# A weight's sign by ScalarE's parametric ReLU, and the norm's factor by one product

## The chip, the cores and the metric

The kernel runs on one core of a Trainium2 chip. The metric is device time in microseconds (us), the median of the runs shown. TensorE multiplies matrices, VectorE and ScalarE work elementwise, GpSimd (POOL in the profile) sets constants and helps with sums, and SyncE (SP) issues the DMAs.

## The reference, cut to what matters

Three stages follow one another, all in float32 at the interface:

```python
# 1. linear attention: batch 8, heads 8, sequence 576, head width 64
kv  = einsum('bhsd,bhse->bhde', k, v)
out = einsum('bhsd,bhde->bhse', q, kv)
rms = sqrt(mean(out * out, axis=-1, keepdims=True) + 1e-06)
x   = (out / rms * g_norm)               # -> 4608 tokens x 512
# 2. gated product
h   = ((x @ w1) * (x @ w2)) @ w3         # 512 -> 1024 -> 1024
x   = h @ w_out                          # 1024 -> 512
# 3. SiLU block
h   = x @ w_in                           # 512 -> 2048
out = (h / (1 + exp(-h))) @ w_out2       # 2048 -> 512
```

Two facts of it touch the change. Every weight matrix reaches the kernel as float64 (pairs of 32-bit words), so the kernel converts each weight to float32 itself. And the root mean square is one number per token and head, which has to be spread over the 64 features of its head before it multiplies `out`.

## The kernel before, in words

**Precision.** A large product runs in three passes on rounded operands: each operand is split into a high part (a ScalarE copy to a rounded type) and a low part (VectorE: operand minus high part), and TensorE adds high*high, high*low and low*high (`passes`, L111). Every pass is 128x128 weights against 128x512 columns.

**Conversion of weights.** The weights come in pieces of 128x512 values, 512 KB each, 72 in all. `advance` (L293) moves a pipeline of pieces by one step and writes the instructions of several pieces in this order: the DMA of piece n+3 (`cv_load`, L154), the high part of piece n-1 on ScalarE (`cv_high`, L207), two scaling operations of piece n+1 on ScalarE (`cv_scale`, L161), the joining of bits of piece n on VectorE (`cv_bits`, L194), and the low part of piece n-1 on VectorE (`cv_low`, L222). In `cv_scale` L169 makes `t` from the high words (scaled by 2^-112) and L170 makes `z` from the low words. In `cv_bits` L201 takes the sign bit of the high word from the raw tile and puts it into `z`, and L203 shifts `t` left by three bits and joins `z`. So VectorE does three operations a piece (L201, L203, the low part) and ScalarE three (L169, L170, the high part). The raw tile has three buffers, and a fourth for every fourth piece of the opening; it is free once its last reader is done, which is L201.

**Opening.** Up to about 88 us the kernel folds w3 and w_out into one matrix (`w_mm`, L476: 16 groups of 12 products, each group waiting for one or two fresh pieces), and fits in the first batches of `kv`, the first 512 tokens of the attention, and the first pieces of w1 and w2. `SLOTS` (L55) writes the order out by hand: it names after which piece each step of the attention stands.

**Middle.** From about 88 to 613 us the gated product runs over seven chunks of 512 tokens (products `pa`, `pb`, `x2ps`), and `event` and `att_step` (L585, L613) place the attention of the other chunks and the rest of the conversion between its products, again in an order written out by hand.

**End.** From there to the end the SiLU block and the remaining gated chunks run as seven-product block schemes (L796), whose weights are reloaded from memory.

**The norm.** For each of nine chunks: `att_c` sums squares with the constant matrix `ones`, so that rows 32p and 32p+1 of one bank hold the two heads of pair p; `att_d` and `att_e` make the factor `u` (ScalarE: Ln, Exp, Square; VectorE: two operations) and split it into `rh` (ScalarE) and `rl` (VectorE). `att_r` (L412), called twice a chunk, spreads it: for two pairs p, one product of 32 rows of `spread` with `rh` and one with `rl`, both into the same bank. `att_x` (VectorE) multiplies by it. `spread` holds -0.5 where a row belongs to a half, set by GpSimd before anything else runs (L128 to L136).

**Order.** Each engine works through its own instructions in the order in which they are written; an instruction that waits holds up all behind it on its engine. SP issues DMAs in the same way.

Of the kernel before, what the change touches and what calls it, by code (L numbers as in the profile page):

```python
# [7 lines left out]
F32 = mybir.dt.float32  # L8
F32R = mybir.dt.float32r
U32 = mybir.dt.uint32  # L10
AF = mybir.ActivationFunctionType
ALU = mybir.AluOpType
# [3 lines left out]
P = 128  # L16
B, H, S, D = 8, 8, 576, 64
# [5 lines left out]
N = 512  # L23
# [50 lines left out]
def fused(ctx, tc, q, k, v, g, w1, w2, w3t, wo1, wb, out):  # L74
# [3 lines left out]
    nc = tc.nc  # L78
    opened = {}

    def pool(name, **how):
        opened[name] = tc.tile_pool(name=name, **how)
        return opened[name].__enter__()
# [9 lines left out]
    const = pool(name="const", bufs=1, side="right")  # L93
# [10 lines left out]
    def bank(tag, bufs, name):  # L104
        return ps.tile([P, N], F32, tag=tag, bufs=bufs, name=name)

    def split(h, l, x):
        nc.scalar.copy(out=h, in_=x)  # L108
        nc.vector.tensor_sub(out=l, in0=x, in1=h.bitcast(F32))
# [11 lines left out]
    eps = const.tile([P, 1], F32)  # L121
    nc.gpsimd.memset(eps, EPS)
    ones = const.tile([P, 32], F32)
    const.tile([P, 80], F32, name="pad_left")
    spread = const.tile([P, P], F32R)
    kv32 = [const.tile([P, KD, D], F32, name=f"kv32_{i}") for i in range(2)]
    const.tile([P, 120], F32, name="pad_right")
# [1 line left out]
    nc.gpsimd.memset(spread.bitcast(F32), 0.0)  # L129
    for i in range(2):  # L130
        nc.gpsimd.memset(ones[i * D:(i + 1) * D, i:i + 1], 1.0)
    for p in range(KD):
        r = 32 * p
        nc.gpsimd.memset(spread[r:r + 2, D:].bitcast(F32), -0.5)
        nc.gpsimd.memset(spread[r:r + 1, D:].bitcast(F32), 0.0)
        nc.gpsimd.memset(spread[r:r + 1, :D].bitcast(F32), -0.5)  # L136

    wch = [wc.tile([P, N], F32R, name=f"wch{m}") for m in range(K1)]
    wcl = [wc.tile([P, N], F32R, name=f"wcl{m}") for m in range(K1)]
# [11 lines left out]
    stage = {}  # L151
# [9 lines left out]
    def cv_scale(n):  # L161

        if n < len(pieces) and pieces[n][0] is not None and pieces[n][1] != "sum":
            t = cv.tile([P, N], F32, tag="t", name=f"t{n}")
            z = cv.tile([P, N], U32, tag="z", bufs=2, name=f"z{n}")
            w = stage[n].rearrange("p (n two) -> p n two", two=2)
            nc.scalar.activation(out=t, in_=w[:, :, 1].bitcast(F32), func=AF.Copy, scale=2.0 ** -112)  # L169
            nc.scalar.activation(out=z, in_=w[:, :, 0], func=AF.Copy, scale=0.93 * 2.0 ** -29)  # L170
            stage[n] = stage[n], t, z

    def cv_sum(n):


        src, _, role, dst = pieces[n]
        t = cv.tile([P, N], F32, tag="t", name=f"t{n}")
        w = N // len(src)
        for x, halves in enumerate(src):
            h, l = (y.bitcast(F32) for y in halves)  # L180
            nc.vector.tensor_add(out=t[:, x * w:(x + 1) * w], in0=h, in1=l)
            for i, y in ((0, h), (1, l)):

                y0, at0 = (0, x * w) if role else (max(0, 2 * P - x * w), max(0, x * w - 2 * P))
                if y0 < w:
                    if w > 2 * P:
                        ops_ = dst[:, 1:3, i, :] if role else dst[:, 0:1, i, :]
                        nc.sync.dma_start(out=ops_, in_=y[:, y0:].rearrange("p (o c) -> p o c", c=2 * P))
                    else:
                        op = 1 + at0 // (2 * P) if role else 0  # L190
                        nc.sync.dma_start(out=dst[:, op, i, at0 % (2 * P):at0 % (2 * P) + w], in_=y)
        stage[n] = t

    def cv_bits(n):  # L194
        if n < len(pieces) and pieces[n][0] is not None and pieces[n][1] == "sum":
            cv_sum(n)
        elif n < len(pieces) and pieces[n][0] is not None:
            raw, t, z = stage[n]
            hi = raw.rearrange("p (n two) -> p n two", two=2)[:, :, 1]
            tu = t.bitcast(U32)  # L200
            nc.vector.scalar_tensor_tensor(out=z, in0=hi, scalar=0x80000000, in1=z,  # L201
                                           op0=ALU.bitwise_and, op1=ALU.bitwise_or)
            nc.vector.scalar_tensor_tensor(out=tu, in0=tu, scalar=3, in1=z,  # L203
                                           op0=ALU.logical_shift_left, op1=ALU.bitwise_or)
            stage[n] = t
# [87 lines left out]
    def advance():  # L293
        nonlocal done
        n = done
        flush()
        cv_load(n + 3)
        cv_high(n - 1)
        cv_scale(n + 1)
        cv_bits(n)  # L300
        block_sums(n)
        cv_low(n - 1)
        done += 1
# [8 lines left out]
    at = pool(name="at", bufs=1)  # L312
# [46 lines left out]
    r_t = {}  # L359
# [42 lines left out]
    def att_e(c):  # L402

        s, r, u = r_t[c]
        nc.vector.scalar_tensor_tensor(out=u, in0=s, scalar=D * EPS, in1=u, op0=ALU.add, op1=ALU.mult)
        nc.vector.scalar_tensor_tensor(out=u, in0=u, scalar=3.0, in1=r, op0=ALU.subtract, op1=ALU.mult)
        h = at.tile([P, N], F32R, tag="sq", bufs=4, name=f"rh{c}")
        l = at.tile([P, N], F32R, tag="sq", bufs=4, name=f"rl{c}")
        split(h, l, u)
        r_t[c] = h, l  # L410

    def att_r(c, i):  # L412

        ps_ = [2 * i, 2 * i + 1]
        banks_ = [bank("att", 2, f"rb{c}_{p}") for p in ps_]
        for n, half_ in enumerate(r_t[c]):
            for p, o in zip(ps_, banks_):
                rows = slice(32 * p, 32 * p + 32)
                nc.tensor.matmul(out=o, lhsT=spread[rows, :], rhs=half_[rows, :], start=n == 0, stop=n == 1,  # L419
                                 skip_group_check=True)  # L420
        for p, o in zip(ps_, banks_):
            sq_t[c, p] = o

# [19 lines left out]
    with tc.tile_pool(name="pro", bufs=2, side="right") as pro:  # L443
# [58 lines left out]
        for i in range(2):  # L502
            for nm, f in (("a", att_a), ("b", att_b), ("r", att_r), ("x", att_x), ("f", att_f)):
                at_slot(SLOTS[nm][i], f, 0, i)
        for nm, f in (("c", att_c), ("d", att_d), ("e", att_e)):
            at_slot(SLOTS[nm][0], f, 0)
# [3 lines left out]
        for n in range(3):  # L510
            cv_load(n)
            for f in slots.pop(n - 3, ()):
                f()
        cv_scale(0)
        for i in range(2):
            nc.sync.dma_start(out=g2[i * D:(i + 1) * D, :], in_=g.rearrange("(d o) -> d o", o=1))
# [72 lines left out]
    for c in range(1, NCH):  # L589
        if 1 < c < B:  # L590
            event(gap, kv_mm, c, [0, 1, 2])
            event(gap, kv_load, c, [3, 4])
            event(gap + 6, kv_mm, c, [3, 4])
            event(gap + 6, kv_out, c)
        if c + 1 < B:
            event(max(gap + 6, 2), kv_load, c + 1, [0, 1, 2])
        if c > 1:
            for p in range(KD):
                event(gap_was + 11, q_load, c, p)
        for i in range(2):  # L600
            event(gap + 7 + 3 * i, att_a, c, i)
            event(gap + 7 + 3 * i, att_b, c, i)
        event(gap + 12, att_c, c)
        event(gap + 13, att_d, c)
        event(gap + 14, att_e, c)
        for i in range(2):
            event(gap + 17 + i, att_r, c, i)
            event(gap + 17 + i, att_x, c, i)
            event(gap + 17.5 + i + 1.5 * (c in LATER), att_f, c, i)
        gap_was = gap  # L610
        gap += 20 if c + 1 < B else 13
# [304 lines left out]
    for b, (u, which, i) in enumerate(blocks):  # L916
        nxt = blocks[b + 1] if b + 1 < len(blocks) else None
        kind, w = UNITS[u]
# [3 lines left out]
        ps_ = {}  # L922
# [88 lines left out]
```

## Time and profile before

| | us |
|---|---|
| median of 3 runs (1421.34 to 1426.93) | 1422.8 |
| the profiled execution | 1423.97 |
| its span, first to last instruction | 1422.2 |
| TensorE busy in the span | 1394.9 (98%) |
| VectorE busy | 865.6 (61%) |
| ScalarE busy | 664.8 (47%) |

| stretch (us) | TensorE busy | VectorE busy | ScalarE busy |
|---|---|---|---|
| 0 to 9 | 0.00 | 2.73 | 5.07 |
| 9 to 16 | 6.31 | 4.88 | 4.39 |
| 88.3 to 104.5 | 14.51 | 6.86 | 8.04 |
| 250 to 552 | 302.00 | 194.45 | 146.04 |
| 640 to 1400 | 759.56 | 460.75 | 340.90 |

A busy time is the union of an engine's instructions in the stretch. Matmuls overlap in the records, so the time that one holds TensorE is read from the distance of two starts, not from its length. The engine whose busy time fills a stretch sets that stretch; where none does, the waits say who was late. PE is TensorE, PEld its weight load, DVE VectorE, ACT ScalarE, SPq the DMA queue of SyncE.

### The profile page before, as it was taken

Reading aid. Unit: us, or ns where it says so; the run is one execution under the profiler, and the core shown is the slowest. Engines: PE = TensorE matmul, PEld = TensorE weight load, DVE = VectorE, ACT = ScalarE, POOL = GpSimd, SP = SyncE. Lnnn points to the kernel's source line nnn. Section 1 sums busy time; section 2 is a strip of 40 time slices with the busy share of each in tenths; the row PEclk is TensorE's granted clock in tenths of the full one; section 3 lists DMA queues with packets and bytes.
Section 4 is the critical chain, followed back from the end, with each engine's and each line's share of the span. In section 5 each row is a group of like instructions: output and inputs, shape, how many; then the busy total and the mean of one; then the engine's idle time right before and its main releaser. Section 6 shows DMA issues by size and latency. Waiting matters only on the chain.

```text
span 1422.2 us, 19310 instructions
## 1 busy us (share of the span) xinstructions
PE 1394.9 (98%) x7112; PEld 1156.3 (81%) x7112; DVE 865.6 (61%) x1263; ACT 664.8 (47%) x1064; POOL 288.0 (20%) x163
## 2 busy tenths in 40 slices
PE   6789999999999999999999999999999999999998
PEld 4567777778777777888888888888888889999998
DVE  7757565665757585243774558455854676567458
ACT  7756544454444553232544445343534354544443
POOL 0000000000000000204352235224522442235222
PEclk9989999999999999999999999999999999999999
DMA  9655666787595776257678666866686668888886
GB/s 331 219 163 165 197 206 219 238 277 253 180 296 169 239 248 207 97 182 229 194 221 284 193 193 195 309 193 193 194 289 203 194 201 282 294 252 263 287 255 200
DMA packets 149726, 320.06 MB, mean 225 GB/s; under 512 B 14208, under 2 KB 72576, under 8 KB 149632
## 3 DMA queue, kind: packets, MB, share of 16 engines
q1 hardware_dynamic: 149056, 317.78, 70.0%
q8 instruction: 57, 0.93, 0.3%
q10 hardware_dynamic: 576, 1.05, 0.2%
q14 instruction: 37, 0.30, 0.1%
HBM read 246.42 MB, written 72.35 MB: 224 GB/s over the span
## 4 chain that ended last, share of the span: by engine, by line
PE 95%; DVE 2%; DMA 1%; ACT 1%; issue 1%; ACTq 0%; DVEq 0%
PE ps L796 57%; PE pb L113 4%; PE x2ps L113 4%; PE pa L113 4%; PE pb L115 4%; PE pb L114 4%; PE x2ps L115 4%; PE x2ps L114 4%; PE pa L115 4%; PE pa L114 4%; PE kvps L338 1%; PE o L370 1%; PE rb L419 1%; DMA raw<-w3t_l 1%; DVE z L201 1%
## 5 line engine op out<-in xcount | busy, mean ns | idle before, releaser
L796 PE MATMUL ps<-xo,w 128*128 128x512 f32 (+1 forms) x2016 | 424.6, 371 | 0.0
L796 PEld LDWEIGHTS ps<-xo,w 128*128 128x128 f32 x2016 | 369.0, 188 | 52.5
L796 PE MATMUL ps<-go,w 128*128 128x512 f32 (+1 forms) x1848 | 387.0, 369 | 0.4 <-issue 0.4
L796 PEld LDWEIGHTS ps<-go,w 128*128 128x128 f32 x1848 | 337.3, 188 | 46.7 <-issue 1.0
L697 DVE TENSOR_TENSOR go<-g,go 128x1024 fp32r<-128x1024 f32 (+1 forms) x110 | 124.9, 1137 | 113.6 <-ACT go L696 112.4
L806 DVE TENSOR_TENSOR c<-ps,c 128x512 f32<-128x512 f32 (+1 forms) x260 | 158.0, 636 | 55.1 <-PE ps L796 52.4
L684 POOL TENSOR_TENSOR x_t<-x2r 128x1024 f32<-128x1024 f32 (+1 forms) x12 | 26.6, 2216 | 567.8 <-DMA x2r<-xd 567.4
L696 ACT CAST go<-g 128x1024 fp32r<-128x1024 f32 (+1 forms) x110 | 104.8, 972 | 46.3 <-PE ps L796 45.1
L684 POOL TENSOR_TENSOR g_t<-g 128x1024 f32<-128x1024 f32 (+1 forms) x44 | 100.8, 2291 | 49.1 <-DVE g L878 44.3
L733 DVE TENSOR_TENSOR asb<-pb,asb 128x512 f32<-128x512 f32 x56 | 38.6, 690 | 110.2 <-PE pb L115 100.1
L684 POOL TENSOR_TENSOR g<-g,g_t 128x1024 f32<-128x1024 f32 (+1 forms) x22 | 48.4, 2199 | 261.4 <-DVE go L697 261.4
L108 ACT CAST ch<-asb 128x512 fp32r<-128x512 f32 x56 | 35.0, 624 | 122.3 <-DVE asb L733 122.3
L113 PE MATMUL pb<-xh,w2h 128*128 128x512 f32 x224 | 89.9, 401 | 0.3 <-ACT w2h L217 0.3
L828 ACT COPY s<-ps 128x512 f32<-128x512 f32 (+1 forms) x40 | 21.7, 544 | 145.0 <-PE ps L796 145.0
L113 PE MATMUL pa<-xh,w1h 128*128 128x512 f32 x224 | 89.3, 399 | 0.0
L115 PE MATMUL pb<-xh,w2l 128*128 128x512 f32 x224 | 88.0, 393 | 1.4 <-DVE w2l L230 1.4
L113 PE MATMUL x2ps<-ch,wch 128*128 128x512 f32 x224 | 89.2, 398 | 0.0
L114 PE MATMUL pb<-xl,w2h 128*128 128x512 f32 x224 | 88.0, 393 | 0.0
L697 DVE TENSOR_TENSOR go<-g_t,go 128x1024 fp32r<-128x1024 f32 (+1 forms) x44 | 75.4, 1714 | 20.6 <-ACT go L696 20.6
L115 PE MATMUL x2ps<-ch,wcl 128*128 128x512 f32 x224 | 87.3, 390 | 0.0
L115 PE MATMUL pa<-xh,w1l 128*128 128x512 f32 x224 | 87.3, 390 | 0.0
L114 PE MATMUL pa<-xl,w1h 128*128 128x512 f32 x224 | 87.3, 390 | 0.0
(114 smaller groups left out, 1889.5 us busy)
## 6 DMA issues: line engine op xcount, KB each, us to landing
w<-wbd SPq DMA_DIRECT2D x322, 512.0 KB, 4.3
wbd<-bh SPq DMA_DIRECT2D x72, 256.0 KB, 2.9
raw<-wb_l SPq DMA_DIRECT2D x32, 512.0 KB, 5.4
wbd<-s SPq DMA_DIRECT2D x56, 256.0 KB, 2.7
q<-q_l SPq DMA_DIRECT2D x36, 256.0 KB, 4.6
raw<-w3t_l SPq DMA_DIRECT2D x16, 512.0 KB, 6.0
k<-k_l SPq DMA_DIRECT2D x32, 256.0 KB, 4.5
v<-v_l SPq DMA_DIRECT2D x32, 256.0 KB, 4.8
```

What stands on the lines that cost most here:

```text
L108: nc.scalar.copy(out=h, in_=x)
L113: nc.tensor.matmul(out=ps_out, lhsT=ah, rhs=bh, start=first, stop=False)
L114: nc.tensor.matmul(out=ps_out, lhsT=ah, rhs=bl, start=False, stop=False)
L115: nc.tensor.matmul(out=ps_out, lhsT=al, rhs=bh, start=False, stop=last)
L201: nc.vector.scalar_tensor_tensor(out=z, in0=hi, scalar=0x80000000, in1=z, op0=ALU.bitwise_and, op1=ALU.bitwise_or)
L684: nc.gpsimd.tensor_tensor(out=x, in0=x if a == place else self.src[a], in1=x if b == place else self.src[b], op=ALU.subtract)
L696: nc.scalar.copy(out=t[:, 0, :, :self.w], in_=x)
L697: self.cuts[n].tensor_tensor(out=t[:, 1, :, :self.w], in0=x, in1=t[:, 0, :, :self.w].bitcast(F32), op=ALU.subtract)
L733: nc.vector.tensor_mul(out=asb, in0=pb, in1=asb)
L796: mm = lambda a, bb, start, stop: nc.tensor.matmul(out=o, lhsT=a, rhs=bb, start=start, stop=stop, skip_group_check=True)
L806: eng.tensor_tensor(out=out_, in0=a, in1=b, op=ALU.add)
L828: nc.scalar.copy(out=t[nm, d], in_=o)
```

## The change

`cv_scale` makes `t` with a parametric ReLU instead of a plain copy: a positive value is scaled by 2^-112, a negative one by 2^-112 times -2^32, which makes it positive with an exponent larger by 32. The shift by three bits in `cv_bits` carries that exponent bit into the sign bit, so L201 is left out, and the raw tile is no longer read by VectorE. For the norm, `ones` gets two more columns, so that each pair has four rows (two heads, twice); VectorE makes one tile `hl` = `u` * `low` - `h`, where `low` is 1 in the second two rows and 0 elsewhere, so that two rows hold -`h` and two `u` - `h`; `spread` gets signs of both kinds, and one product of `hl` takes the place of the two of `rh` and `rl`. GpSimd sets the larger constants with more memsets.

```diff
--- before.py
+++ after.py
@@ -121,7 +121,8 @@
     eps = const.tile([P, 1], F32)
     nc.gpsimd.memset(eps, EPS)
     ones = const.tile([P, 32], F32)
-    const.tile([P, 80], F32, name="pad_left")
+    low = const.tile([P, 1], F32)
+    const.tile([P, 79], F32, name="pad_left")
     spread = const.tile([P, P], F32R)
     kv32 = [const.tile([P, KD, D], F32, name=f"kv32_{i}") for i in range(2)]
     const.tile([P, 120], F32, name="pad_right")
@@ -129,11 +130,16 @@
     nc.gpsimd.memset(spread.bitcast(F32), 0.0)
     for i in range(2):
         nc.gpsimd.memset(ones[i * D:(i + 1) * D, i:i + 1], 1.0)
+        nc.gpsimd.memset(ones[i * D:(i + 1) * D, i + 2:i + 3], 1.0)
+    nc.gpsimd.memset(low, 0.0)
     for p in range(KD):
         r = 32 * p
-        nc.gpsimd.memset(spread[r:r + 2, D:].bitcast(F32), -0.5)
-        nc.gpsimd.memset(spread[r:r + 1, D:].bitcast(F32), 0.0)
-        nc.gpsimd.memset(spread[r:r + 1, :D].bitcast(F32), -0.5)
+        for rows, value in ((4, -0.5), (3, 0.0), (2, 0.5), (1, 0.0)):
+            nc.gpsimd.memset(spread[r:r + rows, D:].bitcast(F32), value)
+        for rows, value in ((3, -0.5), (2, 0.0), (1, 0.5)):
+            nc.gpsimd.memset(spread[r:r + rows, :D].bitcast(F32), value)
+        nc.gpsimd.memset(low[r:r + 4, :], 1.0)
+        nc.gpsimd.memset(low[r:r + 2, :], 0.0)
 
     wch = [wc.tile([P, N], F32R, name=f"wch{m}") for m in range(K1)]
     wcl = [wc.tile([P, N], F32R, name=f"wcl{m}") for m in range(K1)]
@@ -166,9 +172,10 @@
             t = cv.tile([P, N], F32, tag="t", name=f"t{n}")
             z = cv.tile([P, N], U32, tag="z", bufs=2, name=f"z{n}")
             w = stage[n].rearrange("p (n two) -> p n two", two=2)
-            nc.scalar.activation(out=t, in_=w[:, :, 1].bitcast(F32), func=AF.Copy, scale=2.0 ** -112)
+            nc.scalar.activation(out=t, in_=w[:, :, 1].bitcast(F32), func=AF.Prelu, scale=2.0 ** -112,
+                                 alpha=-2.0 ** 32)
             nc.scalar.activation(out=z, in_=w[:, :, 0], func=AF.Copy, scale=0.93 * 2.0 ** -29)
-            stage[n] = stage[n], t, z
+            stage[n] = t, z
 
     def cv_sum(n):
 
@@ -195,11 +202,8 @@
         if n < len(pieces) and pieces[n][0] is not None and pieces[n][1] == "sum":
             cv_sum(n)
         elif n < len(pieces) and pieces[n][0] is not None:
-            raw, t, z = stage[n]
-            hi = raw.rearrange("p (n two) -> p n two", two=2)[:, :, 1]
+            t, z = stage[n]
             tu = t.bitcast(U32)
-            nc.vector.scalar_tensor_tensor(out=z, in0=hi, scalar=0x80000000, in1=z,
-                                           op0=ALU.bitwise_and, op1=ALU.bitwise_or)
             nc.vector.scalar_tensor_tensor(out=tu, in0=tu, scalar=3, in1=z,
                                            op0=ALU.logical_shift_left, op1=ALU.bitwise_or)
             stage[n] = t
@@ -405,19 +409,20 @@
         nc.vector.scalar_tensor_tensor(out=u, in0=s, scalar=D * EPS, in1=u, op0=ALU.add, op1=ALU.mult)
         nc.vector.scalar_tensor_tensor(out=u, in0=u, scalar=3.0, in1=r, op0=ALU.subtract, op1=ALU.mult)
         h = at.tile([P, N], F32R, tag="sq", bufs=4, name=f"rh{c}")
-        l = at.tile([P, N], F32R, tag="sq", bufs=4, name=f"rl{c}")
-        split(h, l, u)
-        r_t[c] = h, l
+        hl = at.tile([P, N], F32R, tag="sq", bufs=4, name=f"rhl{c}")
+        nc.scalar.copy(out=h, in_=u)
+        nc.vector.scalar_tensor_tensor(out=hl, in0=u, scalar=low, in1=h.bitcast(F32),
+                                       op0=ALU.mult, op1=ALU.subtract)
+        r_t[c] = hl
 
     def att_r(c, i):
 
         ps_ = [2 * i, 2 * i + 1]
         banks_ = [bank("att", 2, f"rb{c}_{p}") for p in ps_]
-        for n, half_ in enumerate(r_t[c]):
-            for p, o in zip(ps_, banks_):
-                rows = slice(32 * p, 32 * p + 32)
-                nc.tensor.matmul(out=o, lhsT=spread[rows, :], rhs=half_[rows, :], start=n == 0, stop=n == 1,
-                                 skip_group_check=True)
+        for p, o in zip(ps_, banks_):
+            rows = slice(32 * p, 32 * p + 32)
+            nc.tensor.matmul(out=o, lhsT=spread[rows, :], rhs=r_t[c][rows, :], start=True, stop=True,
+                             skip_group_check=True)
         for p, o in zip(ps_, banks_):
             sq_t[c, p] = o
```

## Rows read from the trace of the kernel before

**Rows 1.** The page's part 1: busy us (share of span) and instructions of each engine.

```profile
PE 1394.9 (98%) x7112; PEld 1156.3 (81%) x7112; DVE 865.6 (61%) x1263; ACT 664.8 (47%) x1064; POOL 288.0 (20%) x163
```

**Rows 2.** Busy time by stretch: us, length, busy of each engine (instructions), clock, DMA share, GB/s.

```profile
16.00:46.00 30.00, 27.37 (x167) 18.42 (x167) 26.55 (x42) 27.55 (x51) 0.00 (x0) 1.00 0.94 322
46.00:88.30 42.30, 33.41 (x192) 23.68 (x191) 30.04 (x47) 26.65 (x47) 0.00 (x0) 0.88 0.58 187
...
104.50:250.00 145.50, 145.50 (x836) 111.93 (x836) 92.81 (x158) 76.89 (x139) 0.00 (x0) 1.00 0.61 199
```

**Rows 3.** TensorE's waits, whole span: for whom, us in total, times, longest.

```profile
PE wps L115 <- DVE w3l L234: 5.2, 3, 2.3
PE wps L114 <- DVE wol L234: 2.0, 4, 1.0
PE wps L113 <- ACT w3h L219: 1.9, 1, 1.9
PE kvps L338 <- DVE wcl L109: 1.5, 1, 1.5
PE pb L115 <- DVE w2l L230: 1.4, 1, 1.4
```

**Rows 4.** Tile z, VectorE's sign operation: ns min/median/max, first and last start.

```profile
L201 DVE SCALAR_TENSOR_TENSOR z<-raw,z x72: 681/685/694, 6.2 to 542.9; 128x512 uint32<-128x512 uint32 x72
```

**Rows 5.** Timeline of VectorE, from 57 to 77: start us, length us, instruction.

```profile
57.78 0.69 DVE L201 SCALAR_TENSOR_TENSOR z<-raw,z 128x512 uint32<-128x512 uint32 x1
...
59.11 0.69 DVE L234 TENSOR_TENSOR w3l<-t,w3h 128x512 fp32r<-128x512 f32 x1
...
72.41 0.68 DVE L201 SCALAR_TENSOR_TENSOR z<-raw,z 128x512 uint32<-128x512 uint32 x1
...
75.59 0.69 DVE L201 SCALAR_TENSOR_TENSOR z<-raw,z 128x512 uint32<-128x512 uint32 x1
...
76.93 0.68 DVE L234 TENSOR_TENSOR w3l<-t,w3h 128x512 fp32r<-128x512 f32 x1
```

**Rows 6.** Busy time by stretch again, three short ones with a low granted clock.

```profile
60.40:63.20 2.80, 2.80 (x8) 2.18 (x7) 1.35 (x2) 2.54 (x5) 0.00 (x0) 0.50 0.85 248
...
77.60:83.60 6.00, 5.94 (x14) 4.68 (x15) 3.89 (x7) 2.99 (x7) 0.00 (x0) 0.50 0.75 238
...
100.30:104.50 4.20, 4.14 (x14) 2.90 (x17) 1.96 (x4) 1.76 (x4) 0.00 (x0) 0.59 0.95 312
```

**Rows 7.** Timeline of TensorE around one call of att_r: start us, length us, instruction.

```profile
125.96 0.50 PE L419 MATMUL rb<-rh,spread 32*128 32x512 f32 x2
126.29 0.40 PE L419 MATMUL rb<-rl,spread 32*128 32x512 f32 x2
126.62 0.50 PE L113 MATMUL pa<-xh,w1h 128*128 128x512 f32 x1
126.95 0.40 PE L114 MATMUL pa<-xl,w1h 128*128 128x512 f32 x1
127.19 0.40 PE L115 MATMUL pa<-xh,w1l 128*128 128x512 f32 x1
```

**Rows 8.** Tile rb, the second products: ns min/median/max, first and last start.

```profile
L419 PE MATMUL rb<-rl,spread x36: 383/392/392, 64.2 to 549.9; 32*128 32x512 f32 x36
```

**Rows 9.** Line L169 by stretch: us, length, ScalarE busy (instructions), clock, DMA share, GB/s.

```profile
16.00:46.00 30.00, 9.51 (x14) 1.00 0.94 322
46.00:104.50 58.50, 8.11 (x12) 0.88 0.54 171
```

**Rows 10.** Groups of ScalarE: line, op, out<-in, count, busy us, mean ns, idle before.

```profile
L169 ACT ACTIVATE t<-raw 128x512 f32<-128x512 f32 x72 | 48.7, 677 | 14.7 <-DMA raw<-wb_l 7.1 <-DMA raw<-w3t_l 5.1 <-DMA raw<-wo_l 2.3
...
L217 ACT ACTIVATE w1h<-t,g 128x512 fp32r<-128x512 f32 x8 | 5.8, 721 | 1.8 <-DVE t L203 1.8
```

**Rows 11.** Line L117, the first load of ScalarE's tables: ns, count, start.

```profile
L117 ACT ACT_TABLE_LOAD  x1: 1283/1283/1283, 0.7 to 0.7; - x1
```

**Rows 12.** SP's queue, 0 to 106 us: waits in total us, times, longest.

```profile
SPq L158 <- DVE z L201: 72.6, 27, 12.3
```

## The prediction

> **What bounds the kernel now.** I read the page's engine totals first. TensorE is busy 1394.9 of 1422.2 us [rows 1]; the reader is to see that only 27.3 us of the span are open to anything that does not shorten TensorE's own work. Then the busy time by stretch shows where those 27.3 us lie: from 104.5 to 250 TensorE is busy 145.50 of 145.50, while from 16 to 46 it is busy 27.37 of 30.00 and from 46 to 88.3 only 33.41 of 42.30 [rows 2]. So the opening is limited by whoever prepares TensorE's operands, and everything after it by TensorE. The waits say who that is: most of what TensorE waits for in the opening is a low part that VectorE makes, 5.2 + 2.0 + 1.5 + 1.4 = 10.1 us, and one wait of 1.9 us is ScalarE's [rows 3]. Last I looked at the granted clock: three short stretches have it near 0.50, the lower of the two levels (1.2 instead of 2.4 GHz) [rows 6], each beginning just after such waits. The VectorE operation that the change removes is on the way of these waits; the product that it removes is on TensorE itself.
>
> **The change part by part.**
>
> *The spreading product.* Each call of att_r loses its second pair of products. The pair with rh starts at 125.96, the pair with rl at 126.29 and the next product of another kind at 126.62 [rows 7]: a pair holds TensorE 0.33 us. There are 36 records of the second kind, two a call [rows 8], so 18 calls, and 18 x 0.33 = 5.9 us go. Were only the streaming of one product saved, it would be the distance of two full products, 127.19 - 126.95 = 0.24 us [rows 7], or 18 x 0.24 = 4.3 us. I take 5.9, since the distance of exactly these two pairs is the nearest row. Nearly all calls lie in the part where TensorE never waits, so nothing gives the time back; the two in the opening bring `ob` earlier by as much, and that is on VectorE's way to the next low part.
>
> *The sign operation.* L201 takes 0.685 us and is run 72 times, 49 us in all [rows 4]. After 104.5 us this is worth nothing: TensorE doesn't wait there [rows 2], and covers it. Before that it counts once for each L201 that stands in VectorE's queue between what VectorE last waited for and the low part that TensorE wants. By wait:
> - The four waits for wol (2.0 us) lie in the piece-by-piece part before 46 us. There ScalarE is busy 27.55 of 30.00 us [rows 2]; as it becomes the next late one, the stretch can give at most 2.45, and the DMAs, at 0.94 of their time, press as well. I take 1.3 (0 to 2.0).
> - The wait for wcl (1.5) has one L201 ahead of it: 0.7.
> - The wait for w3l at 59.8 has one L201 ahead, begun at 57.78 before w3l at 59.11; another about 8 us later is alike; the longest, 2.3 us, has two, at 72.41 and 75.59, before w3l at 76.93 [rows 5]. That is four, 4 x 0.69 = 2.8 of the 5.2.
> - The wait for w2l (1.4): one, 0.7.
> ScalarE's own wait, 1.9 for w3h, stays: it hangs on the chain of the norm (Ln, Exp, Square, two VectorE operations, a copy), which keeps its length. Sum 1.3 + 0.7 + 2.8 + 0.7 = 5.5 us. Low end 2, if ScalarE or a DMA is late instead in most places; high end 7, if the earlier release of the raw tile also takes waits for DMAs away.
>
> *The clock.* In the three stretches of rows 6 TensorE is busy 2.80, 5.94 and 4.14 us at 0.50, 0.50 and 0.59. At the full clock this work would take 1.4, 2.97 and 2.44: the low clock costs 1.4 + 3.0 + 1.7 = 6.1 us. Each stretch follows a bunch of waits that shrinks: ScalarE's 1.9 and one of the two shorter w3l waits, (5.2 - 2.3) / 2 = 1.45, ahead of the first, the 2.3 ahead of the second, the 1.4 for w2l ahead of the third. Ahead of the first 1.9 + 0.75 = 2.65 remain, so I leave it; ahead of the others 0.9 and 0.7 remain, about the size of waits that pass without a loss elsewhere in the opening (a wol wait of 1.0 [rows 3], in a stretch at 1.00 [rows 2]), so I count them as gone: 4.7 us. Bounds 6.1 (all gone) and -3.0 (none gone, and one more like the longest, since the pattern of work moves).
>
> *The parametric ReLU itself.* No row has one. Bounds: L169 now takes 0.677 us; the same shape with its scale read from a tile takes 0.721 (L217) [rows 10]. I take 0.68, no change, the same operand shapes on the same engine being the nearest row; with 0.72, 26 of them before 104.5 [rows 9] add 1.1 us to ScalarE, in the stretch at most 14 x 0.04 = 0.6 against its 2.45 of idle time, so 0.
>
> *What moves.* The raw tile is freed by ScalarE's L170 instead of L201, about one VectorE operation earlier. The queue of SP waited 72.6 us in 27 places for L201 [rows 12]; those loads, and the k, v and q loads behind them, start sooner. It is hidden where the pieces are there in time and is in the 7 above where they are not. `hl` reads one more operand than `rl`, a few hundredths, once a chunk; the extra memsets run on GpSimd at the start, and the constants are wanted after 50 us only. Both 0.
>
> Sum: 5.9 + 5.5 + 4.7 = 16.1. The profiled execution took 1423.97, 1.8 more than its span, so it would take 1407.9; it lies 1.2 above the median of the runs, and from that median I get 1406.7. I predict 1407.
>
> *One rule weighed.* ScalarE loads its tables once in the opening, 1.28 us at 0.7 [rows 11], and then runs Copy, Square, Ln and Exp without another load. The Trainium skill (ScalarE: Activation LUTs, Table sets: the hidden batching unit) says that cheap functions are in every set, but does not name this one; and its section What ACT_TABLE_LOAD costs gives 2.66 us for each switch, with a drain. No row shows a switch between neighbours. By the first sentence nothing is added; by the second, if the function is in another set than Ln and Exp, two switches around the first chunk's norm would make the sum 16.1 - 5.3 = 10.8.
>
> **The rivals.**
> - *The clock does not come back.* The waits shrink but the low level is granted as before. For it: what remains ahead of the first stretch is 2.65 us, and a shift of a few us may put gaps elsewhere. Against: the shorter waits of the opening pass at 1.00. Gain 5.9 + 5.5 = 11.4, time 1411.4.
> - *ScalarE or the DMAs take VectorE's place.* For: ScalarE is busy 27.55 of 30 and the DMAs 0.94 from 16 to 46 [rows 2]. Against: after 46 ScalarE has 15.7 us of 42.3 idle. Then about 1 of the 5.5 is left and the clock stays: 5.9 + 1 = 6.9, time 1416.
> - *A second set of tables.* If the function sits in another set than Ln and Exp, the load of 1.28 [rows 11] stands before Ln and again before the next conversion; for the first chunk both lie on the chain to w3h, the other eight chunks lie where TensorE does not wait. That adds 2.6 and holds one low-clock stretch (3.0): 16.1 - 5.6 = 10.5, time 1412.3. For: only that no row shows it otherwise. Against: Copy and Square run beside Ln with no load.
> - *The product saves nothing,* that is, the change does not do what it says there: TensorE is held by the change of shape into and out of the spreading product and not by the second pair. For: the products around it start 0.33 apart instead of 0.24. Against: the two pairs have the same shape and are still 0.33 apart. Gain 10.2, time 1412.6.
> - *The parametric ReLU is slow* (the other side: slower). If each is x us longer than the copy, the stretch from 16 to 46 grows by 14x - 2.45, and each of the five later waits by about x; the 5.5 and 4.7 are gone. That meets the 5.9 of the product at 19x = 8.35, x = 0.44 us, or an operation of 1.12 us. With twice the copy's time (x = 0.68) it is 10.5 - 5.9 = 4.6 slower, 1427, and 1430 with one more low-clock stretch. Against: L169 and L217, of this shape, lie within 0.05 us of each other, whatever they compute [rows 10].
>
> **How the numbers follow.** Forecast 0.55, own range 1402 to 1412; clock not back 0.20; ScalarE or DMAs in its place 0.12; tables 0.04; product saves nothing 0.04; slow function 0.05. The range goes from 1401 (17 to 22 us saved: high ends 7 and 6.1 with part of a further gain from earlier loads) to 1416, which takes in all but the slow function, half of the third case and the tails. A measurement of this kernel tells about 0.5% (7.1 us) from no change, so the border of faster is 1415.7: the first case, the clock, the tables and the product lie below it, and a third of the third case, 0.87 in all. The rest of the third case and the mild end of the slow function are the same, 0.09; slower 0.04.
>
> **What would show it.** In the profile after: L201 gone and 36 fewer products, TensorE's next product 0.33 us after the first rb pair; L169 near 0.68 us and no table load between; TensorE's waits for VectorE in the opening 10.1 before, about 4.6 after, that for w3h still near 1.9; granted clock near 1.00 around the former 77 and 100 us. The end of the opening (TensorE full) near 94 instead of 104.5 (5.5 + 4.7 + 2 x 0.33 earlier). Wrong would be a longer L169, new waits for ScalarE of more than 3 us, or a low clock elsewhere in the opening.

## The result and the profile after

| | before | after |
|---|---|---|
| median (us) | 1422.07 | 1409.8 |
| runs | 1419.78 to 1426.93, 4 | 1409.34 to 1410.77, 4 |
| profiled execution, span | 1423.97, 1422.2 | 1410.77, 1409.0 |

The ratio is 0.991, 95% interval 0.9883 to 0.9937: faster by 12.3 us, where 16.1 were forecast (1407 against 1409.8, inside the range). Line numbers after L121 are shifted in the changed kernel: L169 is L175, L203 is L207, L419 is L424.

The page's part 1 after (busy us, share, instructions) answers to [rows 1]: TensorE has 36 instructions less, VectorE 72, ScalarE as many as before.

```profile
PE 1386.1 (98%) x7076; PEld 1151.4 (82%) x7076; DVE 818.6 (58%) x1191; ACT 663.0 (47%) x1064; POOL 290.9 (21%) x190
```

Busy time by stretch after, columns as in [rows 2] (TensorE, weight loads, VectorE, ScalarE, GpSimd, granted clock, DMA share, GB/s):

```profile
16.00:46.00 30.00, 27.44 (x153) 18.59 (x154) 17.79 (x28) 27.59 (x52) 0.00 (x0) 1.00 0.96 335
46.00:88.30 42.30, 37.02 (x225) 25.99 (x223) 25.61 (x40) 27.04 (x48) 0.00 (x0) 0.92 0.68 233
...
104.50:250.00 145.50, 145.50 (x817) 112.93 (x816) 85.13 (x148) 74.57 (x136) 0.00 (x0) 1.00 0.59 194
```

The reader is to see two different halves of the opening. From 16 to 46 VectorE fell from 26.55 to 17.79 us, and TensorE gained nothing (27.37, now 27.44); ScalarE, at 27.59 of 30, and the DMAs, at 0.96, are about as full as before. From 46 to 88.3 TensorE rose from 33.41 to 37.02. TensorE's waits after, whole span, answer to [rows 3]:

```profile
PE kvps L342 <- DMA v<-v_l: 10.0, 2, 9.3
PE wps L115 <- DVE w3l L238: 2.1, 3, 0.8
PE wps L113 <- ACT woh L223: 1.9, 2, 1.1
PE wps L113 <- ACT w3h L223: 1.9, 1, 1.9
PE kvps L342 <- DVE wcl L109: 0.9, 1, 0.9
PE wps L114 <- DVE wol L238: 0.8, 3, 0.3
PE pb L115 <- DVE w2l L234: 0.6, 1, 0.6
```

VectorE's four waits of [rows 3] went from 10.1 to 2.1 + 0.9 + 0.8 + 0.6 = 4.4 us. The wait for ScalarE's woh, which was 0.9 before (a row below shows it in a second profile of before), is 1.9, and beside the 9.3 for the first load of v a second wait for v, of 0.7, has come. The parametric ReLU takes no longer than the copy before [rows 10], and ScalarE still loads its tables once in the opening [rows 11]; the row of L169 before, that of L175 after, and that of L117 after:

```profile
L169 ACT ACTIVATE t<-raw x72: 642/675/715, 5.0 to 538.7; 128x512 f32<-128x512 f32 x72
```

```profile
L175 ACT ACTIVATE t<-raw x72: 643/672/765, 4.9 to 526.4; 128x512 f32<-128x512 f32 x72
```

```profile
L117 ACT ACT_TABLE_LOAD  x1: 1283/1283/1283, 0.7 to 0.7; - x1
```

One call of att_r in the middle, first TensorE's products, then its weight loads (start us, length us), answers to [rows 7]:

```profile
120.10 0.39 PE L115 MATMUL pa<-xh,w1l 128*128 128x512 f32 x1
120.42 0.49 PE L424 MATMUL rb<-rhl,spread 32*128 32x512 f32 x2
120.84 0.50 PE L113 MATMUL pb<-xh,w2h 128*128 128x512 f32 x1
```

```profile
120.42 0.18 PEld L424 LDWEIGHTS rb<-rhl,spread 32*128 32x128 f32 x2 [0.35 <-issue]
120.84 0.19 PEld L113 LDWEIGHTS pb<-xh,w2h 128*128 128x128 f32 x1 [0.24 <-issue]
120.95 0.19 PEld L114 LDWEIGHTS pb<-xl,w2h 128*128 128x128 f32 x1
```

The single pair holds TensorE 0.42 us, the two pairs before held it 0.66: 0.24 saved a call. The weight load of the next product of full shape begins at 120.84, at the same moment as the product, while a load between products of one shape runs ahead (120.95 for a product at 121.18).

A useful mark for what follows is the first x2ps product: it stands where the opening ends, and from it on TensorE hardly waits. By the rows of tile x2ps, before and then after (ns min/median/max, first and last start us), it moved from 105.5 to 96.6, so 8.9 us came in the opening; from first to last x2ps it took 506.8 us before and 502.8 after, so 4.0 in the middle.

```profile
L113 PE MATMUL x2ps<-ch,wch x224: 389/389/499, 105.5 to 612.3; 128*128 128x512 f32 x112
```

```profile
L113 PE MATMUL x2ps<-ch,wch x224: 389/389/501, 96.6 to 599.4; 128*128 128x512 f32 x112
```

Apart from the rb products both kernels run the same products in the same order on TensorE, so the 8.9 us can be followed by the starts of one and the same product (us, first profiles):

| the product | before | after | ahead by |
|---|---|---|---|
| a `wps` shortly ahead of 46 us | 43.12 | 42.42 | 0.70 |
| `kvps`, behind the wait for wcl | 50.66 | 49.43 | 1.23 |
| `wps`, behind the first wait for w3l | 59.85 | 57.98 | 1.87 |
| `wps`, behind the second | 67.94 | 65.91 | 2.03 |
| `wps`, behind the third | 77.66 | 73.94 | 3.72 |
| `wps`, behind the low clock of before | 84.01 | 77.47 | 6.54 |
| `pb`, behind the wait for w2l | 100.36 | 93.06 | 7.30 |
| first `x2ps` | 105.46 | 96.56 | 8.90 |

### The profile page after: what moved, and what is told of

Its sections match the earlier page's. It is cut to its first block, busy times and chain, and to the rows that moved or that the text cites. A ratio compares the mean times of both kernels' runs of the same rounds, so it can differ in the third digit from the quotient of the medians.

```text
span 1409.0 us, 19167 instructions
## 1 busy us (share of the span) xinstructions
PE 1386.1 (98%) x7076; PEld 1151.4 (82%) x7076; DVE 818.6 (58%) x1191; ACT 663.0 (47%) x1064; POOL 290.9 (21%) x190
## 4 chain that ended last, share of the span: by engine, by line
PE 95%; ACT 2%; DMA 1%; DVE 1%; issue 1%; SPq 0%; ACTq 0%; DVEq 0%
PE ps L801 57%; PE x2ps L113 4%; PE pb L113 4%; PE pa L113 4%; PE pb L115 4%; PE x2ps L114 4%; PE x2ps L115 4%; PE pb L114 4%; PE pa L114 4%; PE pa L115 4%; DMA raw<-w3t_l 1%; PE kvps L342 1%; PE o L374 1%; PE s L393 1%; PE rb L424 1%
## 5 line engine op out<-in xcount | busy, mean ns | idle before, releaser
L114 PE MATMUL x2ps<-cl,wch 128*128 128x512 f32 x224 | 87.3, 390 | 0.0
```

The costliest lines, as they stand in the source:

```text
L114: nc.tensor.matmul(out=ps_out, lhsT=ah, rhs=bl, start=False, stop=False)
```

## Experiments

| kernel | median us (runs) | x2ps first, last start | products at the low clock, 57 to 108 us |
|---|---|---|---|
| before | 1422.07 (4) | 105.5, 612.3 | 27 |
| before, second and third profile | 1420.4, 1427.16 | 101.9, 608.7; 108.7, 615.5 | 14, 40 |
| after | 1409.8 (4) | 96.6, 599.4 | 10 |
| after, second profile | 1411.4 | 97.2, 600.1 | 10 |
| sign only | 1414.06 (5) | 96.0, 602.8 | 6 |
| product only | 1417.51 (12) | 102.5, 606.2 | 14 |
| operation back, opening | 1416.33 (5) | 101.9, 604.9 | 14 |
| the same, reading raw | 1417.11 (10) | 103.4, 606.4 | 17 |
| operation back, later | 1411.23 (4) | 96.0, 599.7 | 7 |
| three pairs | 1418.3 (9) | 95.9, 606.1 | 0 |
| factor later | 1406.8 (4) | 92.5, 595.4 | 0 |
| factor later and copies | 1405.49 (4) | 90.9, 593.8 | 0 |

The last column counts the products of full shape in the profiled execution whose records are 0.6 us or longer; they follow each other at 0.43 us instead of 0.23.

**The sign alone.** The kernel before with this and without L201:

```diff
-nc.scalar.activation(out=t, in_=w[:, :, 1].bitcast(F32), func=AF.Copy, scale=2.0 ** -112)
+nc.scalar.activation(out=t, in_=w[:, :, 1].bitcast(F32), func=AF.Prelu, scale=2.0 ** -112, alpha=-2.0 ** 32)
```

> Only the sign's part of the change (parametric ReLU, no L201); the norm's factor is spread as before. Theory (the opening gains by VectorE's shorter queue and by the low-clock stretches that then stay away, 8.4 us; the product is worth 0.24 us a call): the first x2ps product starts near 97.0 us (105.46 before, 96.56 after), the middle keeps its length, time 8.5 us below before. Rival 1 (the product makes most of the gain, by 0.33 us a call and by starting the chain of the norm earlier): at most 5 us below before. Rival 2 (the two parts need each other, since the rb products lie on VectorE's way in the opening): first x2ps near 100.

Measured: ratio to before 0.9938 (0.9922 to 0.9955), 8.1 us; x2ps starts at 96.0, and the middle is 602.8 - 96.0 = 506.8 us as before. By these profiles the gain of the opening is the sign's, and the parts do not need each other there.

**The product alone.** The changed kernel with the plain copy and L201 back:

> Only the norm's part of the change (one product from hl); L201 and the plain copy stay. Theory: 18 calls of 0.24 us, 4.3 us below before, the first x2ps product near 105, the next product 0.42 us behind the rb pair. Rival (a pair is worth the 0.33 us that stood between two starts before, as the prediction has it): 5.9 us below before. Rival 2 (the part moves the opening's waits and its low-clock stretches as well): first x2ps moves by more than 1 us either way.

Measured: 0.997 (0.9959 to 0.9982), 4.7 us, which lies between the two prices. The distance behind the rb pair is 0.43, as expected, and the middle is 503.7 us instead of 506.8, so that 3.1 of the 4.7 lie there. The start of x2ps at 102.5 was not expected and fits rival 2, but the product is not seen to cause it: the long waits for VectorE are those of before (w3l 5.4, wcl 1.5, w2l 1.4), and the low clock differs, as it does between profiles of the kernel before itself (below).

**VectorE's operation put back, in the opening and later.**

```diff
+if n < 29:       # the other kernel: n >= 29
+    nc.vector.scalar_tensor_tensor(out=z, in0=z, scalar=0, in1=z, op0=ALU.bitwise_or, op1=ALU.bitwise_or)
 nc.vector.scalar_tensor_tensor(out=tu, in0=tu, scalar=3, in1=z, ...
```

> The changed kernel, with a VectorE operation of L201's form put back on z for the first 29 pieces (it joins z with itself and changes nothing); it does not read the raw tile, which is still freed by ScalarE. Theory (VectorE's time in the opening is what counts): the first x2ps product is back near 104.5, the low granted clock near 77 and 100 us is back, time about 8 us above the changed kernel. Rival (the gain comes from the raw tile, freed earlier, so that loads start earlier): at most 2 us above the changed kernel.

Measured: 1416.33, 6.5 us above the changed kernel; w3l is back at 5.4, wcl 1.5, w2l 1.4. VectorE's time in the opening it is, and not the loads. The first x2ps came at 101.9 and not near the 104.5 expected, mostly since the clock came out otherwise: low again near 60 and 77, but not at 100, where the wait of 1.4 is back all the same.

> The changed kernel, with the same VectorE operation put back for pieces 29 to 71 only. Theory: 43 operations, 29 us of VectorE, of which only the first few lie before TensorE is full: 0 to 1 us above the changed kernel (the wait for w2l near 93 us grows from 0.6 to about 1.3). Rival (VectorE's time counts in the middle too, there as waits that the records of TensorE do not show): 3 us or more above it.

Measured: 1411.23, 1.4 us above. The changed kernel itself took 1411.4 in its second profile, so the time does not tell the two apart; the traces do, and at another place than expected: the wait for w2l stayed at 0.6, and the middle is 503.7 us instead of 502.8 (502.9 in the second profile). The cause shows in one chunk of this kernel (start us, length us; VectorE's multiplication of the first call, then TensorE's second call):

```profile
181.42 1.28 DVE L434 TENSOR_TENSOR ob<-rb,ob 128x512 f32<-128x512 f32 x2
...
182.55 0.70 PE L427 MATMUL rb<-rhl,spread 32*128 32x512 f32 x2
...
183.18 0.50 PE L113 MATMUL pa<-xh,w1h 128*128 128x512 f32 x1
```

The second call writes the banks that the first call's multiplication reads until 182.70, and so holds TensorE 0.63 instead of 0.43. Three of the 16 calls take 0.63 to 0.77 in this way, none in the changed kernel; the product-only kernel has the same three (0.62 to 0.75, and 503.7 us). So a shorter pair makes the bank late unless VectorE is relieved as well.

**Who frees the raw tile.**

```diff
-    nc.vector.scalar_tensor_tensor(out=z, in0=z, scalar=0, in1=z, op0=ALU.bitwise_or, op1=ALU.bitwise_or)
+    nc.vector.scalar_tensor_tensor(out=z, in0=hi, scalar=0, in1=z, op0=ALU.bitwise_and, op1=ALU.bitwise_or)
```

> As the kernel with the VectorE operation put back for the first 29 pieces, but the operation now reads the high words of the raw tile as well (masked to nothing), so that the raw tile is freed by VectorE as before the change. Theory (the earlier release of the raw tile is worth little, since up to 46 us ScalarE and the DMAs are full either way): 0 to 1 us above that kernel (1416.3). Rival (the loads started late before): 2 us or more above it, and more of TensorE's waits for wol.

Measured: 1417.11 (1415.82 to 1418.7) against 1416.33 (1416.12 to 1416.8), 0.8 us, the expected size, though the ranges overlap. The waits for wol are 2.4 instead of 0.9, but they are 2.0, 0.8 and 2.1 in the three profiles of before (below), so this difference shows nothing.

**The price of a pair.** The pair is issued three times into the same banks:

```diff
+for _ in range(3):
     for p, o in zip(ps_, banks_):
```

> The changed kernel, with each call of att_r issuing its pair of products three times into the same banks (the second and third write the same values again). It measures what one more pair costs TensorE. Theory (a pair between two others costs its 0.24 us; the 0.42 us from a pair to the next product of full shape holds a weight load that is not done ahead): 2 x 18 x 0.24 = 8.6 us above the changed kernel, rb starts 0.24 apart. Rival (a pair costs the 0.33 us that stood between the starts before): 2 x 18 x 0.33 = 11.9 us above.

Measured: 1418.3, 8.5 us above the changed kernel.

```profile
120.21 0.96 PE L425 MATMUL rb<-rhl,spread 32*128 32x512 f32 x6
121.10 0.50 PE L113 MATMUL pb<-xh,w2h 128*128 128x512 f32 x1
```

Three pairs and the way out take 0.89 us against 0.42 for one, so (0.89 - 0.42) / 2 = 0.235 a pair. The theory's price holds. The starts, expected 0.24 apart, are 0.33 and 0.22 apart, so the distance of two starts is not the price of a pair: one pair holds TensorE 0.42, two 0.66, three 0.89.

**The profile of before, again.**

> The kernel before, unchanged, profiled a second time. Theory (the low-clock stretches of the opening differ from execution to execution at the same waits): waits of TensorE within 0.5 us of those shown, but stretches at 0.50 of another length or number, and the first x2ps product moved by 1 us or more from 105.46. Rival (they follow the waits): the same three stretches, x2ps within 0.5 us.

> The kernel before, profiled a third time. Theory: the same waits once more, first x2ps product anywhere from 101 to 106, by the number of products at the low clock (27 between 59 and 104 us in the first profile, 14 in the second, 0.2 us each). Rival: 101.9 as in the second, the first profile being the odd one.

Measured: most of the waits are the same, here TensorE's in the second profile,

```profile
PE wps L115 <- DVE w3l L234: 5.2, 3, 2.3
PE wps L113 <- ACT w3h L219: 1.9, 1, 1.9
PE kvps L338 <- DVE wcl L109: 1.5, 1, 1.5
PE pb L115 <- DVE w2l L230: 1.4, 1, 1.4
PE wps L113 <- ACT woh L219: 0.9, 1, 0.9
PE wps L114 <- DVE wol L234: 0.8, 3, 0.4
```

but two differ by more than the expected 0.5 us. The waits for wol are 0.8 here and 2.1 in the third profile, where the first had 2.0. In the third those for w3l are 3.9 instead of 5.2, because TensorE, at the low clock from 60 us on, came later to the second of them and waited 0.25 instead of 1.56:

```profile
PE wps L115 <- DVE w3l L234: 3.9, 3, 2.3
```

```profile
69.39 0.80 PE L115 MATMUL wps<-woh,w3l 128*128 128x512 f32 x1 [0.25 <-DVE w3l L234]
```

The clock is another one each time. The low stretches of the second and of the third profile (columns as in [rows 6]):

```profile
60.00:63.00 3.00, 3.00 (x8) 1.89 (x6) 1.09 (x2) 2.25 (x4) 0.00 (x0) 0.50 0.79 251
76.70:80.50 3.80, 3.57 (x9) 2.80 (x10) 3.37 (x6) 1.48 (x3) 0.00 (x0) 0.55 0.83 235
```

```profile
60.00:65.00 5.00, 4.70 (x12) 3.28 (x12) 2.20 (x4) 3.39 (x6) 0.00 (x0) 0.50 0.73 225
67.70:73.00 5.30, 5.05 (x17) 3.47 (x14) 4.70 (x8) 3.27 (x6) 0.00 (x0) 0.50 0.48 124
80.70:86.70 6.00, 5.79 (x14) 4.53 (x15) 4.04 (x7) 3.00 (x6) 0.00 (x0) 0.50 0.74 247
104.00:107.20 3.20, 3.20 (x9) 2.45 (x8) 1.48 (x3) 1.28 (x3) 0.00 (x0) 0.50 0.92 333
```

Worked out as in the prediction they cost 3.0 x 0.5 + 3.57 x 0.45 = 3.1 us and (4.70 + 5.05 + 5.79 + 3.20) x 0.5 = 9.4 us; the first profile had 6.1. (In the third the clock is at 0.50 between the first two rows too, for 2.7 us of TensorE's time, which costs up to 1.4; the shorter wait for w3l gives 1.3 back.) The x2ps starts, 101.9, 108.7 and 105.5, are about as far apart; 108.7 lies outside the 101 to 106 that were expected. The runs say the same: each has its mean granted clock on record, and the kernel before took 1417.6 to 1418.7 us in its four runs at 1.000, 1419.1 to 1420.4 in seven at 0.999, 1420.5 to 1421.2 in six at 0.997, and 1426.8 and 1427.0 in two at 0.991.

> The changed kernel, unchanged, profiled a second time. Theory (the low clock differs between executions at the same waits): waits for VectorE and ScalarE within 0.5 us of the first profile's, but the low stretch behind 58 us shorter than its 6.7 us or gone, the first x2ps product between 95 and 97.5. Rival (the low clock follows the waits): the same stretch.

Measured: the waits are the first profile's within 0.2 us, with one more, for a load of q:

```profile
PE o L374 <- DMA q<-q_l: 0.8, 1, 0.8
```

The stretch did not go: 10 products again, and this part of the expectation failed. The stretch in the second profile and in the first:

```profile
58.50:64.50 6.00, 5.93 (x24) 4.08 (x26) 1.82 (x4) 3.00 (x6) 0.00 (x0) 0.50 0.82 223
```

```profile
58.00:64.70 6.70, 6.70 (x44) 4.79 (x44) 2.52 (x5) 3.50 (x8) 0.00 (x0) 0.54 0.80 243
```

That is 3.0 and 3.1 us. That it can be missing at the same waits is shown by the kernel with three pairs, whose waits ahead of it are 1.9 and 0.8 too:

```profile
56.00:66.00 10.00, 7.18 (x58) 4.94 (x58) 7.00 (x12) 8.62 (x15) 0.00 (x0) 1.00 0.58 185
```

Over all thirteen profiles the low clock is less a matter of chance than the three of one kernel suggest. Six of them run VectorE's operation in the opening (before three times, product only, and the two with the operation back there), seven do not. The third wait for w3l, near 77 and 74 us in the first profiles, is of one size in each group:

```profile
77.66 0.79 PE L115 MATMUL wps<-woh,w3l 128*128 128x512 f32 x1 [2.27 <-DVE w3l L234]
```

```profile
73.94 0.50 PE L115 MATMUL wps<-woh,w3l 128*128 128x512 f32 x1 [0.82 <-DVE w3l L238]
```

| TensorE's wait (us) | profiles that have it | with the low clock in it or right behind |
|---|---|---|
| third for w3l, 2.27 or 2.28 | 6 | 6 |
| third for w3l, 0.82 or 0.83 | 7 | 0 |
| second for w3l, 1.53 to 1.56 | 5 | 0 |
| 1.9 for w3h, then first for w3l, 1.40 to 1.55 | 6 | 6 |
| 1.9 for w3h, then first for w3l, 0.68 to 0.82 | 5 | 4 |
| for w2l, 1.36 | 6 | 2 |
| for w2l, 0.64 | 7 | 0 |

The two profiles missing where w3h is waited for are those of the last two kernels below, which have no such wait.

At equal granted clock the runs also tell the clock's share in the gain. Before, the kernel took 1419.8, 1420.7 and 1420.9 us in the mean at 0.999, 0.998 and 0.997 (seven, two and six runs); the changed kernel took 1409.3, 1410.1 and 1411.4 (one, three and one). That is 9.5 to 10.6 us of gain without the clock, so some 2 of the 12.3 are the clock's, an estimate from few runs of the changed kernel.

**What is left: the place of the factor.**

```diff
-    "e": (18.5,),
+    "e": (19,),
```

> The changed kernel, with att_e of the first chunk one place later in the order written out by hand (behind the next step of the conversion instead of ahead of it). Theory (what is left of the opening's waits after the change is ScalarE's queue: w3h stands behind the copy rh, which waits for VectorE): TensorE's wait for w3h falls from 1.9 to under 0.4 us and that for w3l behind it from 0.8 to under 0.5; 2 to 3 us below the changed kernel, and up to 2 more if the low granted clock of 58 to 65 us goes as well. Rival (the factor is then late itself: the rb product waits as long as w3h did): within 1 us of the changed kernel.

Measured: 1406.8 (ratio to before 0.989, 0.9875 to 0.9905), 3.0 us below the changed kernel. ScalarE's queue, first of the changed kernel and then of this one, shows why:

```profile
55.23 0.62 ACT L413 CAST rh<-u 128x512 fp32r<-128x512 f32 x1 [1.48 <-DVE u L410]
55.75 0.61 ACT L223 CAST w3h<-t 128x512 fp32r<-128x512 f32 x1
```

```profile
53.89 0.60 ACT L223 CAST w3h<-t 128x512 fp32r<-128x512 f32 x1
...
56.58 0.62 ACT L413 CAST rh<-u 128x512 fp32r<-128x512 f32 x1 [0.95 <-DVE u L410]
```

w3h needs nothing of the norm; it stood behind rh. Now its wait is gone, and TensorE waits 0.3 for the factor instead. The first wait for w3l, 0.8, is gone too, as expected; but the second grew from 0.45 to 1.24 and the third stays at 0.82, so w3l costs 2.1 in all as in the changed kernel. The low stretch does not occur in this profile, and all four runs have a mean granted clock of 1.000, where those of the changed kernel have 0.997 to 0.999. Part of the gain is the clock's, then: the product behind the first wait for w3l starts at 57.98 in the changed kernel and at 55.27 here, that behind the second at 65.91 and 61.79. So the waits give 2.7 us, the second wait takes 0.8 back, and some 2.2 of the 4.1 us between the profiles are the low stretch.

**And the copies.** As that, and

```diff
+if c == 0:
+    nc.vector.tensor_copy(out=ob, in_=o)
+else:
     nc.scalar.copy(out=ob, in_=o)
```

> As the kernel with att_e later, and the copies ob of the first chunk on VectorE instead of ScalarE. Theory (VectorE has room in the opening since the change, 17.79 of 30 us busy, and ScalarE has none, 27.59): the wait for woh near 37 us falls from 1.1 to under 0.3, 0.8 us below the kernel with att_e later alone. Rival (the DMAs set the pace up to 46 us): the same time, the wait reappears as one for a load.

Measured: 1405.49 (0.988, 0.9865 to 0.9896), 1.3 us below, the fastest version here. The wait of 1.1 for woh near 37 us is gone, but a wait of 1.04 for wol stands at 37.9 in its place, since VectorE now makes the copies ahead of it. What was gained lies in several places, each of a few tenths (wcl 0.9, now 0.3; woh near 16 us 0.8, now 0.2), and the loads, at 0.99 of their time from 16 to 46, may explain some of it; the runs do not settle which.

## Why the prediction was right, step by step

**What bounds the kernel** held: the two gains lie where it put them, in the opening and in TensorE's own work of the middle. The parts add up about as terms of a sum do: sign 8.1 and product 4.7 us alone, 12.8 in sum, and 12.3 together; but the 4.7 hold a shift of the opening that the product does not explain, and the middle alone gives 3.1. All three terms were too large, and no error made up for another: the range of 1402 to 1412 took them in. Of the signs named beforehand two did not come: the next product 0.33 us behind the rb pair (it is 0.42), and the end of the opening 10.5 us earlier (x2ps came 8.9 earlier).

**The product** was mis-sized: 5.9 forecast, 4.3 by the traces (18 x 0.24), the lower of the two values that were weighed. The step that failed is "I take 5.9, since the distance of exactly these two pairs is the nearest row". Of the 0.66 us that a call held TensorE, the second 0.33 was the way from a pair to the next product of another shape, with the weight load that does not run ahead. That way stays, whichever pair comes last, and is 0.42 behind a single pair. The rival in which the product saves nothing had this mechanism right and its price too high.

**The sign operation, VectorE's part,** was right behind 46 us: 4.2 forecast, 4.5 less wait in the first profiles, with the operations counted wait by wait (w3l 3.1 for 2.8, wcl 0.6 for 0.7, w2l 0.8 for 0.7). Ahead of 46 us the 1.3 for wol matched the first profiles (1.2) by luck: wol moves between 0.8 and 2.1 in before alone, and is 0.8 and 0.6 after. What was not in the sum is what became late next, ScalarE's woh by 1.0 and a load by 0.7. The product that starts at 43.12 in the first profile of before starts at 42.48 and 43.76 in the others, and at 42.42 and 43.02 in the two of after: 0.4 us earlier in the mean, which is inside that scatter. The rival "ScalarE or the DMAs take VectorE's place" came true up to 46 us, where TensorE's busy time did not move, and not after.

**ScalarE's wait of 1.9** stayed, as forecast, but the reason given was half of it. w3h hung on the chain of the norm only because it stood behind the chain's copy rh in ScalarE's queue; one step in that order removed the wait.

**The clock** was over-sized: 4.7 forecast from one profile. The mechanism held where the forecast leaned on the longest wait: the low stretch near 77 follows the wait of 2.27 in all six profiles that have it, and the wait of 0.82 in none of seven. The stretch near 100 was the luck of the profile it was priced from; it occurs in two of six. The one near 60 was left as it was, but grew from 7 to 10 products. Between the two first profiles the low clock gave back 2.8 us near 77 and 1.6 near 100, by the table of starts, and took some 0.9 near 60, where the lead grew by 0.16 although the wait for w3l behind it was 1.1 shorter: 3.5. By runs of equal granted clock about 2 of the 12.3 are its share. Over three profiles of before the low clock cost 6.1, 3.1 and 9.4 us, 6.2 in the mean, over two of after 3.1 and 3.0, so one profile could not price it.

The first profiles lie 13.2 us apart in span, and these add up: 0.7 up to 43 us, 8.2 from there to x2ps (some 4.4 of waits for VectorE, 3.5 of clock, the rest the two calls of att_r there and small differences), 4.0 in the middle and 0.3 behind it. Without the clock that is 9.7, which fits the 9.5 to 10.6 of the runs.

**The costs put at nothing** held for the parametric ReLU (median 0.672 us, where the copy's was 0.675), for the tables, for the raw tile (0.8 us between the medians), and for `hl`, whose operation takes 0.752 us where that of rl took 0.692, once a chunk. "After 104.5 us this is worth nothing" is true of the kernel before. It is off by 0.9 us for the changed one, where the shorter pair leaves less time for the bank to come free.

## What to carry to other kernels

Price a removed instruction by what its neighbours then cost, not by its distance to them: between products of two shapes the way out is paid once, however many there are. Where one engine's queue is shortened, find what is queued next on the others before counting its waits as gained; here a third of VectorE's work went from 16 to 46 us and TensorE's busy time stayed, with ScalarE and the DMAs as full as before. And take the clock's part of a time from several profiles of the same kernel, or from runs of equal granted clock.

## What the runs showed of the hardware

A parametric ReLU with an immediate slope costs what a scaled copy costs, 0.672 us against 0.675 for 128x512, and ran in the opening beside Ln and Exp without a further load of tables. TensorE's granted clock fell to 1.2 GHz in or right behind one wait of 2.27 us, or behind waits of 1.9 and 1.4 to 1.55 us close together, in every profile that had them (six each). The size of a single wait does not settle it: behind one of 1.36 us it fell in two of six profiles, behind one of 1.55 us in none of five, and behind 1.9 and 0.7 to 0.8 in four of five; behind the waits of 0.64 and 0.82 us that stand by themselves it never did (seven each). In the two last versions, whose longest wait behind 46 us is 1.2 us, it did not fall there, and all eight of their runs have a mean clock of 1.000. The Trainium skill (TensorE: Matmul & The Clock Gate, Part 1: The HAM clock gate) says of the slow products of a kernel's start that their number varies from run to run of one kernel. Here it was 9, 9 and 8 in the three profiles of before (from 10 to 15 us) and 5 and 6 in the two of after, so it varied by one; the products of the later stretches, of which that sentence does not speak, were 27, 14 and 40.
